# A fused attention, MoE and cosine-MLP kernel: another order for its first cells, other load places, GpSimd work in pieces

## The chip, the cores and the metric

The kernel runs on one core of a Trainium2 chip. The metric is the device time of one execution in microseconds (us). Three runs of the kernel before took 1261.51, 1262.10 and 1262.34 us; the median is 1262.1 us. One further execution was recorded by the hardware profiler.

## The reference

Three layers in a row, all in float32. The first is a linear attention with a decaying state (4 batches, 8 heads, 768 steps, head size 48):

```python
for t in range(S):
    kt, vt, rt = (k[:, :, t], v[:, :, t], r[:, :, t])
    cur = np.einsum('bhd,bhe->bhde', u[None] * kt, vt)
    y[:, :, t] = np.einsum('bhd,bhde->bhe', rt, state + cur)
    state = w[None, :, :, None] * state + np.einsum('bhd,bhe->bhde', kt, vt)
```

Its output, as 3072 tokens of 384 values, goes through a mixture of four experts (`out += p[:, e] * (relu(x @ w1[e]) @ w2[e])`, 1024 wide, p the normalised probabilities) and then through an MLP of width 2048, `(h * cos(h)) @ w_out` with `h = x @ w_in`.

## The kernel before, in words

**Work.** The tokens are cut into six blocks of 512 columns, the hidden layers into units of 8 slices of 128 rows. The program is a list of *items*, numbered n: one weight slice against one token block (256 or 512 columns). An item is an up-projection into a PSUM bank `hp` (two banks, taken in turn, n even and n odd), an evacuation by ScalarE (`gh`, the relu) and VectorE (`gl`, the remainder of the split into two float32r parts), and two items later a down-projection into three banks `a`. Items 0 to 7 use plain float32 with the raw weights (`raw_load(q)` loads those of item q); from item 8 on each product is three float32r matmuls of split operands, so each weight slice is loaded into a staging tile `s` (three of them), then split by ScalarE (high part) and by VectorE or, on odd n, GpSimd (low part). Items 8 to 15 use weight keys 0 to 7; key k is split some items ahead of item 8 + k.

**Attention.** It is cut into 24 *cells* of 128 steps (b, i). The first two are computed ahead of item 0 in a beginning of their own: scores (`b_score`), masks (`b_mask`), products with v (`b_in`), copy to SBUF (`b_y`), transposes to the layout of x (`b_x`). The others are mixed into the items by a table: `ONE_AT[c]` is the item in which cell c's matmuls run (`a_one`), every fourth item up to item 26, every third after it. For each cell p = `ONE_AT[c-1]` sets when the preparing steps are issued: `a_kt` and `a_ru` on GpSimd, `a_r`, `a_rk`, `a_kp` and `a_sum` on VectorE. The matmuls of `a_one` need kp, r, the k table and, since they also write an `hp` bank, the end of the evacuation of the item before. The cell's result goes to DRAM in four stores (`yd`) and comes back as x.

**What sets the order.** Every engine runs its own list in the order in which the program issues it, and a DMA issued by ScalarE stands in ScalarE's list behind the activations before it; the same holds for the loads and stores in SyncE's list. A wait at the head of a list holds everything behind it.

**Names and lines of the steps below.** L728 the dummy matmuls (`warm`), L216 and L225 scores, L239 and L240 mask, L206 `b_ru`, L267 `b_y`, L274 and L275 `b_x` (transposes and the copy to x), L791 and L796 the decay table `table`, `table2`, L589 up-projection of items 0 to 7, L595 to L597 up-projection later, L604 and L608 relu, L609 `gl`, L497 `raw_load`, L493 load of `s`, L504 and L505 weight split, L149 `a_kt`, L153 `a_ru`, L157 `a_rk`, L166 `a_kp`, L161 `a_sum`, L402 the `yd` stores, L693 the GpSimd addition to `acc`.

Of the kernel before, what the change touches and what calls it, by code (L numbers as in the profile page):

```python
# [26 lines left out]
def attention_moe_cos_mlp_kernel(  # L27
# [207 lines left out]
    def b_mask(c):  # L235
        s_ = t_p.tile([128, 2, HP, C], F32, tag="s", name="s")
        by = ld[c]["ps"].rearrange("q c (p a t) -> q a c p t", p=HP, a=2)
        wide = [128, 2, HP, C]
        nc.vector.tensor_tensor(out=s_, in0=by[:, 0], in1=mask.unsqueeze(1).unsqueeze(1).to_broadcast(wide), op=ALU.mult)  # L239
        nc.vector.copy_predicated(  # L240
            out=s_, mask=eye.bitcast(I32).unsqueeze(1).unsqueeze(1).to_broadcast(wide), data=by[:, 1],
        )
        ld[c]["s"] = s_

    def b_in(c, ps):
        d = ld[c]
        tok, s_, so = d["tok"], d["s"], d["so"]
        d["ps_y"] = ps
        for p in range(HP):
            for ch in range(2):  # L250
                for par in range(2):
                    x0, a0 = 64 * (ch ^ par), 64 * ch
                    nc.tensor.matmul(
                        ps[a0:a0 + 64, par, p * D:p * D + D], s_[x0:x0 + 64, ch, p, :], tok[x0:x0 + 64, 4 + ch, p, :],
                        start=p == 0, stop=ch == 0, skip_group_check=True,
                    )
# [239 lines left out]
    def raw_load(q, eng=None):  # L496
        (eng or nc.sync).dma_start(out=raw_w[0, 0, q], in_=moe_wb[q])  # L497

    def w_split(key, eng=None):
        ps, un, q = key  # L500
        t = wp_.tile([128, 2, 2 * DM], F32R, tag="w", name="w")
        if un < NU1:
            src = staged.pop(key)
# [134 lines left out]
    def m_down(n):  # L638
# [10 lines left out]
        def part(t):  # L649
# [128 lines left out]
            double(n)  # L778
            n *= 2

    def tails():
        for a in range(2):
            x = slice(64 * a, 64 * a + 64)
            for ch in range(2):
                last = 2 * C - 1 - C * (ch ^ a)
                nc.scalar.activation(out=tk[x, :, ch], in_=pw[x, :, last:last - C if last >= C else None:-1], func=ACTF.Copy)

    def table():
        pt = ps_d.tile([128, TB], F32, tag="up", name="pt").rearrange("q (p a e) -> q a p e", p=HP, a=2)
# [94 lines left out]
    with tc.manual_schedule():  # L884
# [21 lines left out]
        off = x_bank()
        b_score(0, pair_ps, off[:, 0:HP * C])
        b_off(0)
        tails()
        b_mask(0)  # L910
        b_score(1, dense_ps[0], off[:, HP * C:2 * HP * C])
        b_off(1)
        b_mask(1)
# [2 lines left out]
        b_in(0, dense_ps[1][:, :, 0:HD])
        b_y(0)
        pt = table()
        table2(pt, 0)
        table2(pt, 1)  # L920
        b_in(1, pair_ps[:, :, 0:HD])
        b_y(1)
        b_x(0, dense_ps[0][:, 0])
        b_x(1, dense_ps[0][:, 1])
# [313 lines left out]
```

## Time and profile before

| | |
|---|---|
| median of three runs | 1262.1 us |
| profiled execution, device time | 1262.03 us |
| its span, first to last instruction | 1260.3 us |
| outside the span | 1.73 us |
| granted TensorE clock over the span | 0.999 |

The profile's page gives the busy time of each engine; the view of waits says for which engine's instruction a named engine stood idle; the timeline lists single instructions with start, duration and, in brackets, idle time and its releaser. PE is TensorE, DVE VectorE, ACT ScalarE, POOL GpSimd, SP SyncE; a q behind an engine's name is its queue of DMA issues. Times count from the span's start.

### The profile page before, as it was taken

What the parts mean: (1) busy time and instruction counts of PE and PEld (TensorE: products, weight loads), DVE (VectorE), ACT (ScalarE), POOL (GpSimd) and SP (SyncE); (2) the same over time, 40 slices, a digit from 0 to 9 for tenths busy, and PEclk for the clock granted to TensorE, in tenths of its full rate; (3) what the DMA queues carried; (4) which work ended last, traced back from release to release, by engine and by line L of the source; (5) the groups of instructions that cost most, each with busy time, mean ns of one, the idle gap of its engine ahead of it and who ended that gap; (6) DMA issues with size and microseconds to landing.
All of it is one profiled execution on the core that took longest, in us unless ns stands there. A gap on an engine that the chain in (4) does not pass through costs nothing.

```text
span 1260.3 us, 20498 instructions
## 1 busy us (share of the span) xinstructions
PE 1246.5 (99%) x8453; PEld 1038.8 (82%) x8453; DVE 773.0 (61%) x1259; ACT 492.9 (39%) x879; POOL 193.6 (15%) x190
## 2 busy tenths in 40 slices
PE   9999999999999999999999999999999999999997
PEld 7898888788888888888888888888888888888886
DVE  6897747766264464546645543326776777777665
ACT  4442313223221131112111222216777677767774
POOL 3664323421100000111111111112000100010100
PEclk9999999999999999999999999999999999999999
DMA  8635634444242243223331410123001400160601
GB/s 322 220 117 177 196 125 154 124 137 111 84 139 59 84 134 109 67 76 127 107 92 52 133 43 9 59 78 122 1 1 42 160 26 25 36 203 13 196 11 47
DMA packets 72501, 126.53 MB, mean 100 GB/s; under 512 B 23153, under 2 KB 44754, under 8 KB 72402
## 3 DMA queue, kind: packets, MB, share of 16 engines
q1 hardware_dynamic: 65634, 93.38, 23.6%
q0 software_dynamic: 4608, 25.17, 6.4%
q10 hardware_dynamic: 2160, 6.62, 1.5%
q8 instruction: 67, 1.10, 0.4%
q14 instruction: 32, 0.26, 0.1%
HBM read 101.90 MB, written 23.25 MB: 99 GB/s over the span
## 4 chain that ended last, share of the span: by engine, by line


## 5 line engine op out<-in xcount | busy, mean ns | idle before, releaser
L595 PE MATMUL hp<-xh,w 128*128 128x512 f32 (+1 forms) x888 | 341.3, 384 | 1.6 <-DVE gl L609 1.6
L596 PE MATMUL hp<-xl,w 128*128 128x512 f32 (+1 forms) x888 | 338.1, 381 | 0.5 <-DVE xl L118 0.5
L597 PE MATMUL hp<-xh,w 128*128 128x512 f32 (+1 forms) x888 | 337.9, 380 | 0.2 <-issue 0.2
L670 PE MATMUL a<-gh,w 128*128 128x512 f32 (+1 forms) x880 | 335.0, 381 | 0.0
L671 PE MATMUL a<-gh,w 128*128 128x512 f32 (+1 forms) x880 | 334.8, 380 | 0.0
L672 PE MATMUL a<-gl,w 128*128 128x512 f32 (+1 forms) x880 | 334.7, 380 | 0.0
L608 ACT ACTIVATE gh<-hp 128x512 fp32r<-128x512 f32 (+1 forms) x200 | 114.5, 573 | 539.7 <-PE hp L597 532.6
L609 DVE SCALAR_TENSOR_TENSOR gl<-hp,gh 128x512 fp32r<-128x512 f32 (+1 forms) x200 | 131.1, 657 | 299.5 <-ACT gh L608 298.8
L595 PEld LDWEIGHTS hp<-xh,w 128*128 128x128 f32 x888 | 166.9, 188 | 35.7 <-DVE gl L609 2.9
L597 PEld LDWEIGHTS hp<-xh,w 128*128 128x128 f32 x888 | 166.9, 188 | 32.1
L596 PEld LDWEIGHTS hp<-xl,w 128*128 128x128 f32 x888 | 167.0, 188 | 31.9 <-DVE xl L118 0.7
L670 PEld LDWEIGHTS a<-gh,w 128*128 128x128 f32 x880 | 165.5, 188 | 32.0 <-ACT rr L626 0.4
L672 PEld LDWEIGHTS a<-gl,w 128*128 128x128 f32 x880 | 165.5, 188 | 31.7
L671 PEld LDWEIGHTS a<-gh,w 128*128 128x128 f32 x880 | 165.5, 188 | 31.5
L693 POOL TENSOR_TENSOR acc<-acc,pm 128x512 f32<-128x512 f32 (+1 forms) x57 | 72.5, 1302 | 537.9 <-DVE pm L692 537.9
L628 DVE SCALAR_TENSOR_TENSOR hs<-rr,hs 128x512 f32<-128x512 f32 x96 | 67.4, 702 | 62.8 <-ACT rr L627 62.8
L626 ACT ACTIVATE rr<-rr 128x512 f32<-128x512 f32 x96 | 60.8, 633 | 86.4 <-DVE rr L621 86.4
L620 DVE SCALAR_TENSOR_TENSOR rr<-ni,hs 128x512 f32<-128x512 int32 x96 | 66.3, 691 | 45.6 <-ACT ni L619 45.6
L621 DVE SCALAR_TENSOR_TENSOR rr<-ni,rr 128x512 f32<-128x512 int32 x96 | 66.5, 692 | 3.3
L507 POOL DMA_DIRECT2D w<-dec_all x32 | 17.1, 535 | 333.0 <-PE a L672 332.1
L118 DVE TENSOR_TENSOR gl<-hs,gh 128x512 fp32r<-128x512 f32 x96 | 66.0, 688 | 0.7 <-ACT gh L117 0.7
L618 ACT ACTIVATE hs<-hp 128x512 f32<-128x512 f32 x96 | 57.2, 596 | 17.8 <-PE hp L597 17.6
(151 smaller groups left out, 1066.2 us busy)
## 6 DMA issues: line engine op xcount, KB each, us to landing
w<-dec_all POOLq DMA_DIRECT2D x32, 768.0 KB, 4.6
s<-in_moe_wb_dram SPq DMA_DIRECT2D x53, 384.0 KB, 4.0
draw<-in_moe_wb_dram SPq DMA_DIRECT2D x32, 384.0 KB, 4.3
dec_all<-dout SPq DMA_DIRECT2D x32, 384.0 KB, 3.0
tok<-in_tok_ch_dram SPq DMA_DIRECT2D x19, 576.0 KB, 5.4
rkt<-in_rkt_dram SPq DMA_DIRECT2D x21, 512.0 KB, 3.8
pb<-pn SPq DMA_DIRECT2D x24, 256.0 KB, 5.0
out_dram<-acc SPq DMA_DIRECT2D x17, 256.0 KB, 2.5
```

Source lines behind the costliest of these rows:

```text
L595: nc.tensor.matmul(hp, wh[:, kk, :], x_h[:, kk, :], start=kk == 0, stop=False)
L596: nc.tensor.matmul(hp, wh[:, kk, :], x_l[:, kk, :], start=False, stop=False)
L597: nc.tensor.matmul(hp, wl[:, kk, :], x_h[:, kk, :], start=False, stop=kk == KD - 1)
L608: nc.scalar.activation(out=gh, in_=hp, func=ACTF.Relu)
L609: nc.vector.scalar_tensor_tensor(out=gl, in0=hp, scalar=0.0, in1=gh.bitcast(F32), op0=ALU.max, op1=ALU.subtract)
L620: nc.vector.scalar_tensor_tensor(out=rr, in0=ni, scalar=-PI2_HI, in1=hs, op0=ALU.mult, op1=ALU.add)
L621: nc.vector.scalar_tensor_tensor(out=rr, in0=ni, scalar=-PI2_LO, in1=rr, op0=ALU.mult, op1=ALU.add)
L628: nc.vector.scalar_tensor_tensor(out=hs, in0=rr, scalar=1.0, in1=hs, op0=ALU.subtract, op1=ALU.mult)
L670: nc.tensor.matmul(a, wh[:, ds], gh, start=q == 0, stop=False)
L671: nc.tensor.matmul(a, wl[:, ds], gh, start=False, stop=False)
L672: nc.tensor.matmul(a, wh[:, ds], gl, start=False, stop=q == BLK - 1)
L693: nc.gpsimd.tensor_tensor(out=o, in0=o, in1=m, op=ALU.add)
```

## The change

Five things change.

1. **The beginning.** The two cells' score remainders and the products of the second cell's last two heads get PSUM banks of their own (`off`, `late`); the mask of the second cell and its products are done in two halves; the copies to x are shared between ScalarE and VectorE and stand ahead of `a_r(2)`; the decay table moves into item 1; 13 dummy matmuls instead of 17, and the two dummy matmuls ahead of item 0 become ScalarE copies.
2. **Loads on ScalarE.** None before item 2. The raw weights of item 3 load at item 2 (before: at item 0), those of 4 and 5 at item 3, of 6 at item 4, of 7 at item 5. Cell 3's loads move to item 2. The raw weights of item 2, loaded by SP, go ahead of the probabilities.
3. **Weight splits of keys 0 to 7** come two items later (n - 5 instead of n - 3), their loads with them.
4. **Cell steps.** Cell 2 runs in item 3 (before: 2); `a_rk` runs at p + 1 for cells three items apart, `a_kp` one item later for cells four items apart; the pieces of x of two blocks are spread over other items.
5. **GpSimd in pieces.** `a_kt` two, `a_ru` two, the weight split three, the addition to `acc` one per 256 columns.

```diff
     def a_kt(c, eng=None):
-        t = ld[c]["t"][:, 1]
-        (eng or nc.gpsimd).tensor_tensor(out=t, in0=t, in1=pw[:, :, 127::-1], op=ALU.mult)
+        for h in (slice(0, HP),) if eng else (slice(0, 2), slice(2, HP)):
+            t = ld[c]["t"][:, 1, h]
+            (eng or nc.gpsimd).tensor_tensor(out=t, in0=t, in1=pw[:, h, 127::-1], op=ALU.mult)
...
     ONE_AT = {c: 4 * c - 6 for c in range(N_FIRST, 9)}
+    ONE_AT[N_FIRST] = 3
...
-        yield from ((a_kt, p), (a_r, p + wide), (a_rk, p + 2), (a_kp, p + 2), (a_sum, p + 2 + wide))
+        yield from ((a_kt, p), (a_r, p + wide), (a_rk, p + 1 + wide), (a_kp, p + 2 + wide), (a_sum, p + 2 + wide))
...
-            (eng or nc.vector).tensor_tensor(out=t[:, 1], in0=src, in1=t[:, 0].bitcast(F32), op=ALU.subtract)
+            n = 3 if eng else 1
+            for x in range(n):
+                cols = slice(x * 2 * DM // n, (x + 1) * 2 * DM // n)
+                (eng or nc.vector).tensor_tensor(
+                    out=t[:, 1, cols], in0=src[:, cols], in1=t[:, 0, cols].bitcast(F32), op=ALU.subtract
+                )
...
-            nc.gpsimd.tensor_tensor(out=o, in0=o, in1=m, op=ALU.add)
+            for x in range(0, width(n), 256):
+                nc.gpsimd.tensor_tensor(out=o[:, x:x + 256], in0=o[:, x:x + 256], in1=m[:, x:x + 256], op=ALU.add)
...
-    XT_LAG = 2
+    XT_LAG = 1
-    WARM_FIRST = 17
+    WARM_FIRST = 13
...
         raw_load(1)
+        raw_load(2)
         prob_load()
-        raw_load(2)
...
+        b_mask(0, 0, HP)
+        b_mask(1, 0, 2)
+        b_mask(1, 2, HP)
         a_ru(2)
         a_kt(2)
...
+        late = (x_bank(), ps_d.tile([128, TB], F32, tag="up", name="late"))
+        y0, y1 = dense_ps[1][:, :, 0:HD], pair_ps[:, :, 0:HD]
+        b_in(0, (y0[:, 0], y0[:, 1]), 0, HP)
+        b_y(0, y0, 0, HP)
+        b_in(1, (y1[:, 0], y1[:, 1]), 0, 2)
+        b_y(1, y1, 0, 2)
+        b_in(1, late, 2, HP)
+        b_x(0, dense_ps[1][:, 0], 0, KD)
+        b_x(1, dense_ps[1][:, 1], 0, 1)
+        b_y(1, late, 2, HP)
+        b_x(1, dense_ps[0][:, 0], 1, KD)
+        b_xc(0, dense_ps[1][:, 0], 0, KD, nc.scalar.activation)
+        b_xc(1, dense_ps[1][:, 1], 0, 1, b_copy)
+        b_xc(1, dense_ps[0][:, 0], 1, KD, b_copy)
         a_r(2)
...
-            if n < BLK - 3:
-                raw_load(n + 3, nc.scalar)
-            if 2 <= n < BLK:
-                w_loads(n - 1)
-                w_splits(n - 3, nc.gpsimd if n % 2 else None)
+            for q in {2: (3,), 3: (4, 5), 4: (6,), 5: (7,)}.get(n, ()):
+                raw_load(q, nc.scalar)
+            if 4 <= n < BLK:
+                w_loads(n - 3)
+                w_splits(n - 5, nc.gpsimd if n % 2 else None)
+            if n == 1:
+                pt = table()
+                for a in range(2):
+                    table2(pt, a)
+                for c in range(N_FIRST + 1):
+                    a_kp(c)
...
-                    w_splits(min(BLK * (g + 1) + w_ahead(n, g), n - 3 if n < BLK + 3 else len(w_keys)), nc.gpsimd if n < 28 and n % 2 else None)
+                    w_splits(min(BLK * (g + 1) + w_ahead(n, g), n - 5 if n < BLK + 6 else len(w_keys)), nc.gpsimd if n < 28 and n % 2 else None)
                     w_loads(w_ns[0] + 2)
```

**ScalarE, from the last copy to x to item 2.** Before (`acc_106` is x, `hp_354` and `hp_355` the two up banks, `gh` the relu of an item):

```order
L267 ACTIVATE yo<-pair_ps 128x2x4x48
L275 ACTIVATE acc_106<-ds_ps 128x3x128 x2
L497 DMA raw_xl_101<-in_moe_wb_dram 128x768
L137 DMA tok<-in_tok_ch_dram 128x1152
L128 DMA rkt<-in_rkt_dram 128x1024
L604 ACTIVATE gh<-hp_354 128x256
L497 DMA raw_xh_102<-in_moe_wb_dram 128x768
```

and now (`hp_350`, `hp_351` are the up banks):

```order
L291 ACTIVATE acc_106<-dy_ps 128x3x128
L970 ACTIVATE hp_351<-wu_b 128x256
L627 ACTIVATE gh<-hp_350 128x256
L970 ACTIVATE hp_350<-wu_b 128x256
L820 ACTIVATE wk_ch<-px 64x384 x2
L627 ACTIVATE gh<-hp_351 128x256
L515 DMA raw_xl_101<-in_moe_wb_dram 128x768
L137 DMA tok<-in_tok_ch_dram 128x1152
L128 DMA rkt<-in_rkt_dram 128x1024
L627 ACTIVATE gh<-hp_350 128x256
```

The load of item 3's raw weights (`raw_xl_101`) stood ahead of item 0's relu; it now stands behind item 1's relu, and the loads of cell 3 (`tok`, `rkt`) behind it.

**SyncE, items 6 to 12, up to the second group of `yd` stores (cell 4's, item 10).** Before, the rows with `s` are the loads of weight keys 3 to 7:

```order
L493 DMA s<-in_moe_wb_dram 128x768 x2
L402 DMA yd_605<-yt 48x4x64 x4
L493 DMA s<-in_moe_wb_dram 128x768
L824 DMA pb<-pn 128x4x128 x2
L493 DMA s<-in_moe_wb_dram 128x768
L137 DMA tok<-in_tok_ch_dram 128x1152
L493 DMA s<-in_moe_wb_dram 128x768
L402 DMA yd_605<-yt 48x4x64 x4
L128 DMA rkt<-in_rkt_dram 128x1024
```

and now:

```order
L511 DMA s<-in_moe_wb_dram 128x768
L848 DMA pb<-pn 128x4x128 x2
L511 DMA s<-in_moe_wb_dram 128x768
L137 DMA tok<-in_tok_ch_dram 128x1152
L511 DMA s<-in_moe_wb_dram 128x768
L419 DMA yd_604<-yt 48x4x64 x4
L128 DMA rkt<-in_rkt_dram 128x1024
L511 DMA s<-in_moe_wb_dram 128x768
L432 DMA acc_104<-yd_604 128x3x256
L511 DMA s<-in_moe_wb_dram 128x768
```

Five `s` loads stood ahead of the second group of `yd` stores; now three do, and keys 6 and 7 stand behind those stores.

**VectorE, items 10 to 13, around the relu remainders of items 12 and 13.** Before (`gl<-hp_354` of even, `gl<-hp_355` of odd items; `kp` and `dsum` are of cell 5):

```order
L609 SCALAR_TENSOR_TENSOR gl<-hp_354,gh 128x256
L505 TENSOR_TENSOR w<-s,w 128x768
L145 TENSOR_TENSOR rkt<-rkt,pw 128x512
L609 SCALAR_TENSOR_TENSOR gl<-hp_355,gh 128x256
L157 TENSOR_TENSOR tok<-tok 128x384
L166 TENSOR_TENSOR kp_127<-tok,wk_ch 128x384
L609 SCALAR_TENSOR_TENSOR gl<-hp_354,gh 128x256
L161 TENSOR_REDUCE dsum<-tok 128x8
L609 SCALAR_TENSOR_TENSOR gl<-hp_355,gh 128x256
```

and now (`hp_350` even, `hp_351` odd):

```order
L632 SCALAR_TENSOR_TENSOR gl<-hp_350,gh 128x256
L526 TENSOR_TENSOR w<-s,w 128x768
L145 TENSOR_TENSOR rkt<-rkt,pw 128x512
L632 SCALAR_TENSOR_TENSOR gl<-hp_351,gh 128x256
L159 TENSOR_TENSOR tok<-tok 128x384
L632 SCALAR_TENSOR_TENSOR gl<-hp_350,gh 128x256
L526 TENSOR_TENSOR w<-s,w 128x768
L168 TENSOR_TENSOR kp_127<-tok,wk_ch 128x384
L163 TENSOR_REDUCE dsum<-tok 128x8
L632 SCALAR_TENSOR_TENSOR gl<-hp_351,gh 128x256
```

`kp` stood ahead of item 12's `gl`; it now stands behind it, but with the split of key 6 (the second `w<-s,w`) ahead of `kp` and of item 13's `gl`.

## Rows read from the trace of the kernel before

**Rows 1.** The page: busy time of each engine, share of the span, instructions.

```profile
PE 1246.5 (99%) x8453; PEld 1038.8 (82%) x8453; DVE 773.0 (61%) x1259; ACT 492.9 (39%) x879; POOL 193.6 (15%) x190
```

**Rows 2.** Waits of PE, whole span: who for whom, us in total, times, longest.

```profile
PE hp L595 <- DVE gl L609: 1.6, 3, 1.1
...
PE hp L357 <- DVE gl L609: 1.1, 2, 0.7
PE pair_ps L177 <- DVE kp L166: 0.9, 1, 0.9
PE ds_ps L274 <- ACT acc L275: 0.6, 1, 0.6
PE hp L934 <- ACT acc L275: 0.6, 1, 0.6
PE hp L596 <- DVE xl L118: 0.5, 1, 0.5
```

**Rows 3.** Timeline of PE: start, duration, line, tiles, count.

```profile
1.34 5.80 PE L728 MATMUL hp<-wu_b,wu_a 128*128 128x512 bf16 x17 [1.34 <-DVE wu_b L887]
...
10.98 0.66 PE L791 MATMUL pt<-ident,acc 128*128 128x128 f32 x4
...
12.44 0.28 PE L259 MATMUL pair_ps<-tok,acc 64*64 64x48 f32 x4
...
13.83 0.55 PE L274 MATMUL ds_ps<-ident,yo 128*128 128x128 f32 x3 [0.63 <-ACT acc L275]
14.95 0.38 PE L934 MATMUL hp<-wu_b,wu_a 128*128 128x256 bf16 x2 [0.58 <-ACT acc L275]
15.17 2.75 PE L589 MATMUL hp<-acc,raw_xh 128*128 128x256 f32 x12
...
37.19 0.47 PE L595 MATMUL hp<-xh,w 128*128 128x256 f32 x1
```

**Rows 4.** Timeline of the beginning, ACT.

```profile
6.07 2.45 ACT L206 ACTIVATE acc<-acc,uw 128x128 f32<-128x128 f32 x8 [3.74 <-DVE acc L199]
```

**Rows 5.** Timeline of the beginning, DVE.

```profile
10.45 0.73 DVE L240 COPY_PREDICATED s<-eye,ds_ps 128x512 f32<-128x512 int32 x1
```

**Rows 6.** Raw weights of item 1, one tile's view: the issue, its time to landing.

```profile
L497 SPq DMA_DIRECT2D raw_xh<-in_moe_wb_dram x1: 328/328/328, 7.1 to 7.1; - x1
...
DMA to landing us min/median/max: 8.5/8.5/8.5
```

**Rows 7.** Raw weights of item 3, the same view.

```profile
L497 ACTq DMA_DIRECT2D raw_xl<-in_moe_wb_dram x1: 378/378/378, 14.4 to 14.4; - x1
...
DMA to landing us min/median/max: 3.2/3.2/3.2
```

**Rows 8.** Timeline of ACT at the end of item 0's up-projection.

```profile
16.73 0.38 ACT L604 ACTIVATE gh<-hp 128x256 f32<-128x256 f32 x1 [1.82 <-PE hp L589]
16.75 0.33 ACTq L497 DMA_DIRECT2D raw_xh<-in_moe_wb_dram  x1
```

**Rows 9.** Timeline of DVE around item 14.

```profile
48.30 0.96 DVE L505 TENSOR_TENSOR w<-s,w 128x768 fp32r<-128x768 f32 x1 [0.31 <-ACT w L504]
...
51.56 2.19 DVE L166 TENSOR_TENSOR kp<-tok,wk_ch 128x384 f32<-128x384 f32 x1
53.67 0.41 DVE L609 SCALAR_TENSOR_TENSOR gl<-hp,gh 128x256 fp32r<-128x256 f32 x1
54.01 0.54 DVE L161 TENSOR_REDUCE dsum<-tok 128x8 f32<-128x384 f32 x1
```

**Rows 10.** Timeline of POOL, same stretch.

```profile
51.18 2.16 POOL L505 TENSOR_TENSOR w<-s,w 128x768 fp32r<-128x768 f32 x1
```

**Rows 11.** Timeline of PE, same stretch.

```profile
54.14 0.39 PE L595 MATMUL hp<-xh,w 128*128 128x256 f32 x1 [1.15 <-DVE gl L609]
```

**Rows 12.** Timeline of SP's queue, items 9 to 13.

```profile
41.06 0.38 SPq L493 DMA_DIRECT2D s<-in_moe_wb_dram  x1
47.29 1.78 SPq L402 DMA_DIRECT2D yd<-yt  x4
49.16 1.36 SPq L128 DMA_DIRECT2D rkt<-in_rkt_dram  x1
```

**Rows 13.** All of SP's loads of `s`: time to landing.

```profile
DMA to landing us min/median/max: 2.7/4.0/6.5
```

**Rows 14.** Timeline of ACT, relu of items 12 and 13.

```profile
48.42 0.84 ACT L504 ACTIVATE w<-s 128x768 fp32r<-128x768 f32 x1
49.76 0.39 ACT L608 ACTIVATE gh<-hp 128x256 fp32r<-128x256 f32 x1 [0.49 <-PE hp L597]
51.95 0.39 ACT L608 ACTIVATE gh<-hp 128x256 fp32r<-128x256 f32 x1 [1.81 <-PE hp L597]
```

**Rows 15.** Timeline of DVE ahead of the wait at 236 us.

```profile
233.40 1.64 DVE L157 TENSOR_TENSOR tok<-tok 128x384 f32<-128x384 f32 x1
234.96 1.35 DVE L166 TENSOR_TENSOR kp<-tok,wk_ch 128x384 f32<-128x384 f32 x1
```

**Rows 16.** Timeline of POOL, same stretch.

```profile
230.11 4.51 POOL L693 TENSOR_TENSOR acc<-acc,pm 128x512 f32<-128x512 f32 x3 [3.49 <-DVE pm L692]
```

More of the change, by code (lines that the diff above doesn't have):

```diff
@@ L147, in a_kt @@
     def a_kt(c, eng=None):
-        t = ld[c]["t"][:, 1]
-        (eng or nc.gpsimd).tensor_tensor(out=t, in0=t, in1=pw[:, :, 127::-1], op=ALU.mult)
+        for h in (slice(0, HP),) if eng else (slice(0, 2), slice(2, HP)):
+            t = ld[c]["t"][:, 1, h]
+            (eng or nc.gpsimd).tensor_tensor(out=t, in0=t, in1=pw[:, h, 127::-1], op=ALU.mult)
     def a_ru(c):
-        t = ld[c]["tok"][:, 0:2]
-        nc.gpsimd.tensor_tensor(out=t, in0=t, in1=uu_ch, op=ALU.mult)
+        for ch in range(2):
+            t = ld[c]["tok"][:, ch]
+            nc.gpsimd.tensor_tensor(out=t, in0=t, in1=uu_ch[:, ch], op=ALU.mult)
     def a_rk(c):
@@ L233, in b_off, with b_mask, b_in @@
         ld[c]["so"] = so
-    def b_mask(c):
-        s_ = t_p.tile([128, 2, HP, C], F32, tag="s", name="s")
+    def b_mask(c, p0, p1):
+        if p0 == 0:
+            ld[c]["s"] = t_p.tile([128, HP, 2, C], F32, tag="s", name="s")
+        heads = slice(p0, p1)
+        s_ = ld[c]["s"][:, heads].rearrange("q p c t -> q c p t")
         by = ld[c]["ps"].rearrange("q c (p a t) -> q a c p t", p=HP, a=2)
-        wide = [128, 2, HP, C]
-        nc.vector.tensor_tensor(out=s_, in0=by[:, 0], in1=mask.unsqueeze(1).unsqueeze(1).to_broadcast(wide), op=ALU.mult)
+        wide = [128, 2, p1 - p0, C]
+        nc.vector.tensor_tensor(
+            out=s_, in0=by[:, 0][:, :, heads], in1=mask.unsqueeze(1).unsqueeze(1).to_broadcast(wide), op=ALU.mult
+        )
         nc.vector.copy_predicated(
-            out=s_, mask=eye.bitcast(I32).unsqueeze(1).unsqueeze(1).to_broadcast(wide), data=by[:, 1],
+            out=s_, mask=eye.bitcast(I32).unsqueeze(1).unsqueeze(1).to_broadcast(wide), data=by[:, 1][:, :, heads],
         )
-        ld[c]["s"] = s_
-    def b_in(c, ps):
+    def b_in(c, ps, p0, p1):
         d = ld[c]
         tok, s_, so = d["tok"], d["s"], d["so"]
-        d["ps_y"] = ps
-        for p in range(HP):
+        for p in range(p0, p1):
             for ch in range(2):
@@ L253, in b_in @@
                     nc.tensor.matmul(
[L254 to L255 removed]
+                        ps[par][a0:a0 + 64, p * D:p * D + D], s_[x0:x0 + 64, p, ch, :], tok[x0:x0 + 64, 4 + ch, p, :],
+                        start=p == p0, stop=ch == 0, skip_group_check=True,
                     )
@@ L259, in b_in, with b_y, b_copy, b_x @@
                 nc.tensor.matmul(
-                    ps[64:128, par, p * D:p * D + D], so[x0:x0 + 64, p, :], tok[x0:x0 + 64, 3, p, :],
+                    ps[par][64:128, p * D:p * D + D], so[x0:x0 + 64, p, :], tok[x0:x0 + 64, 3, p, :],
                     start=False, stop=True, skip_group_check=True,
                 )
-    def b_y(c):
-        yo = t_p.tile([128, DM], F32, tag="yo", name="yo", bufs=2)
-        ld[c]["yo"] = yo
+    def b_y(c, ps, p0, p1):
+        if p0 == 0:
+            ld[c]["yo"] = t_p.tile([128, DM], F32, tag="yo", name="yo", bufs=2)
+        yo = ld[c]["yo"][:, p0 * 2 * D:p1 * 2 * D].rearrange("q (p a d) -> q a p d", a=2, d=D)
+        if isinstance(ps, tuple):
+            for a in range(2):
+                (nc.scalar.activation if a == 0 else b_copy)(
+                    out=yo[:, a], in_=ps[a][:, p0 * D:p1 * D].rearrange("q (p d) -> q p d", d=D), func=ACTF.Copy
+                )
+            return
         nc.scalar.activation(
-            out=yo.rearrange("q (p a d) -> q a p d", a=2, d=D),
-            in_=ld[c]["ps_y"].rearrange("q a (p d) -> q a p d", d=D), func=ACTF.Copy,
-        )
-    def b_x(c, px):
-        for kk in range(KD):
+            out=yo, in_=ps[:, :, p0 * D:p1 * D].rearrange("q a (p d) -> q a p d", d=D), func=ACTF.Copy,
+        )
+    def b_copy(out, in_, func):
+        nc.vector.tensor_copy(out=out, in_=in_)
+    def b_x(c, px, k0, k1):
+        for kk in range(k0, k1):
             nc.tensor.transpose(px[:, kk * 128:kk * 128 + 128], ld[c]["yo"][:, kk * 128:kk * 128 + 128], ident)
-        nc.scalar.activation(
-            out=x_raw[:, :, c * 128:c * 128 + 128], in_=px[:, 0:DM].rearrange("q (k t) -> q k t", k=KD), func=ACTF.Copy
+    def b_xc(c, px, k0, k1, copy):
+        copy(
+            out=x_raw[:, k0:k1, c * 128:c * 128 + 128],
+            in_=px[:, k0 * 128:k1 * 128].rearrange("q (k t) -> q k t", t=128), func=ACTF.Copy,
         )
@@ L779, in powers, with tails @@
             n *= 2
-    def tails():
-        for a in range(2):
+    def tails(*halves):
+        for a in halves:
             x = slice(64 * a, 64 * a + 64)
@@ L788, in table @@
     def table():
[L789 removed]
+        pt = x_bank().rearrange("q (p a e) -> q a p e", p=HP, a=2)
         for p in range(HP):
@@ L902, in attention_moe_cos_mlp_kernel @@
             a_kt(c, nc.vector)
-        nc.vector.tensor_tensor(out=w128, in0=pw[:, :, 2 * C:2 * C + 1], in1=pw[:, :, 2 * C:2 * C + 1], op=ALU.mult)
+        tails(0)
         for c in range(N_FIRST):
             b_ru(c)
[L906 to L913, printed above, removed]
+        off = (x_bank(), ps_d.tile([128, TB], F32, tag="up", name="off"))
+        for c in range(N_FIRST):
+            b_score(c, (pair_ps, dense_ps[0])[c], off[c][:, 0:HP * C])
+        for c in range(N_FIRST):
+            b_off(c)
+        tails(1)
+        b_mask(0, 0, HP)
+        b_mask(1, 0, 2)
+        b_mask(1, 2, HP)
         a_ru(2)
         a_kt(2)
[L916 to L924, printed above, removed]
+        late = (x_bank(), ps_d.tile([128, TB], F32, tag="up", name="late"))
[12 more added lines that the diff above has]
+        b_xc(1, dense_ps[0][:, 0], 1, KD, b_copy)
         a_r(2)
+        nc.vector.tensor_tensor(out=w128, in0=pw[:, :, 2 * C:2 * C + 1], in1=pw[:, :, 2 * C:2 * C + 1], op=ALU.mult)
         a_rk(2)
         a_sum(2)
-        for c in range(N_FIRST + 1):
-            a_kp(c)
         ps_d_ctx.close()
@@ L941, in attention_moe_cos_mlp_kernel @@
             moe2 = False
-            if n < BLK - 3:
-                raw_load(n + 3, nc.scalar)
-            if 2 <= n < BLK:
-                w_loads(n - 1)
-                w_splits(n - 3, nc.gpsimd if n % 2 else None)
-            if n == 3:
+            if n < 2:
+                nc.scalar.activation(out=ups2[1 - n][:, 256:512], in_=wu_b[:, 0:256], func=ACTF.Copy)
+            for q in {2: (3,), 3: (4, 5), 4: (6,), 5: (7,)}.get(n, ()):
[5 more added lines that the diff above has]
+                pt = table()
+                for a in range(2):
+                    table2(pt, a)
+                for c in range(N_FIRST + 1):
+                    a_kp(c)
+            if n == 4:
                 prob_norm()
```

9 lines of the change are left out of this document (4 added, 5 removed).

## Prediction

> **What bounds the kernel now.** I read the page's busy shares first: PE works 1246.5 us of a span of 1260.3 us, VectorE 61%, ScalarE 39% [rows 1]. The kernel is bound by TensorE, and the change takes next to nothing out of PE's list that costs time (the dummy matmuls wait for nothing that is computed). So all that it can win is PE's idle time, and all that it can lose is new idle time. The view of waits lists what there is [rows 2]: about 1.2 us for the copies to x ahead of item 0, then 1.6 + 1.1 + 0.9 + 0.5 = 4.1 us for `gl`, `kp` and `xl`. The timeline of PE says where: the beginning up to 15.17, the first matmul of item 0 [rows 3], and 1.15 at 54.14 [rows 11]; the other 2.95 us fall later. Item 8, the first with split weights, starts at 37.19 [rows 3]; what the beginning wins counts only as far as it is still there by then.
>
> **Beginning.** The end of the masks stays: `b_ru` on ScalarE runs 6.07 to 8.52 [rows 4] and still feeds the scores' remainders, and the last mask operation ends at 10.45 + 0.73 = 11.18 [rows 5]; the halves add two operations' overhead, and the scores start a little earlier, so I take 11.1. From there the chain of the second cell is: its last products (about 0.45, as the 0.28 rows around 12.44 stand), copy of y, two transposes (two thirds of 0.55, 0.37), copy to x, item 0. A copy with both handovers is 14.95 - (13.83 + 0.55) = 0.57 [rows 3]. Sum: 11.1 + 0.45 + 0.57 + 0.37 + 0.57 + 0.3 for two engines on one bank and the wait on the slower of two copies = 13.35. That is 15.17 - 13.35 = **-1.8** (bounds -1.2 and -2.2). The table's transposes (0.66), the 0.63 wait for x's copy and the two dummies are what goes. The 13 dummies end about 1.4 us earlier (5.80 / 17 = 0.34 each); a gap of some 0.9 us before the scores is new. [...]
>
> **What loads give back.** Item 0 now starts at 13.35, each item's six matmuls take 1.3 us (a half of 2.75 [rows 3]), and the table (**+0.66**) stands ahead of item 1: wanted at 13.35 + 1.3 + 0.66 = 15.3. But its raw weights land at 7.1 + 8.5 = 15.6 [rows 6], and their issue is not moved: **+0.3** (0 if they land as the next row's do). Then item 1, item 2 and a down-projection, 3 x 1.3: item 3 wants its weights at 19.5. Their load is issued behind item 1's relu, at about 15.6 + 1.3 + 0.25 = 17.15 (an issue goes as soon as the relu ahead begins [rows 8]); with the 3.2 us of the same load before [rows 7] it lands at 20.35: **+0.75**, bounds +0.2 (2.7, the shortest landing of such a load [rows 13]) and +4.1 (6.5). Item 4's load comes one item later with one more in between: **+0.1**. So +1.8 in all, and item 8 starts where it did.
>
> Before, that load was issued at 14.4, ahead of item 0's relu. [...]
>
> **Item 14, the new wait.** Before, PE stood 1.15 us there, since item 13's `gl` (53.67) stood behind a `kp` of 2.19 us [rows 9, 11], which was held by GpSimd's split of 2.16 us [rows 10]. That goes. But the loads of keys 6 and 7, which were issued at about 40 and 41.06, now stand in SP's list behind cell 4's `yd` stores (47.29 + 1.78) and `rkt` (49.16 + 1.36) [rows 12]: issue 49.6 to 50.5. With the median landing of 4.0 [rows 13], key 6 is there at 54.0. ScalarE holds at its split, and with it relu(13), which ran at 51.95 [rows 14]; then ScalarE 0.84 [rows 14], VectorE's split 0.95 and `kp` 0.55 (as the neighbouring row of that width, 0.54) [rows 9]: `kp` is done at 56.35. PE wants it at 53.95 (its wait at 54.14 less 1.15, then about 0.95 of last products and cell work), so it waits 2.4, and up to 0.3 more for `gl(13)`: 2.65 against 1.15, **+1.5**. Bounds: landing 2.7 from 49.6 gives `kp` at 54.65, a wait of 0.7, -0.45; landing 6.5 from 50.5 gives +4.3. Queued behind the wait on ScalarE are relu(13) and key 7's split, on VectorE `kp`, `dsum`, `gl(13)`: all of PE's next item.
>
> **Later waits.** The waits at 62, 87, 108, 236 and 237 us have one pattern: VectorE's two-input operations stretch beside long GpSimd ones (at 233.40, `a_rk` 1.64 and `kp` 1.35 [rows 15] beside three additions of 1.5 each [rows 16]), and `gl` comes late. Pieces of 256 columns or a third of a weight take 0.7 us, so a VectorE operation is held half as long, `a_rk` starts an item earlier and `kp` stands behind `gl`. Of 2.95 us I take **-2.5** (bounds -2.95 and 0, since no row shows two pieces back to back).
>
> The row shows `kp` stretched from 0.55 to 2.19 and ending 0.41 after the GpSimd operation. [...]
>
> Splits of keys 0 to 5 two items later cost nothing: items 8 to 13 come after them by several us, and ScalarE is idle there. The extra GpSimd overhead is covered, POOL being busy 15% [rows 1].
>
> **Sum.** -1.8 + 1.8 + 1.5 - 2.5 = -1.0. The profiled execution took 1262.03 us, 0.07 below the median, so both give **1261.0 us**.
>
> **Rivals.**
> 1. *The loads come in time.* Item 1's and 3's at the short end, key 6's too: -1.8 + 0.66 + 0.2 - 0.45 - 2.5 = -3.9, **1258.1 us**. For it: the shortest landing 2.7, and ScalarE's and SP's lists hold fewer loads side by side then. Against: the median of 4.0, and that `yd` waits for cell 4's result, which nothing makes earlier.
> 2. *Slower: the loads that were moved back land at the long end*, 6.0 us after their issue, as some loads of `s` do (maximum 6.5 [rows 13]), since items 2 to 5 now issue raw weights, cell loads and key loads in a bunch, and items 10 to 12 stores, `rkt` and keys. Item 3 waits until 23.15 (+2.8 more than above), item 14's `kp` comes 2.0 later: -1.0 + 4.8 = +3.8, **1265.8 us**. It decides from about 0.5 us over my landings at both places; below that the sum stays under the time before. Against it: item 3's load is the first of its bunch, so it should land fast.
> [...]
>
> **How the numbers follow.** 0.2% (2.5 us) is about what a measurement can tell from no change: faster is under 1259.6, slower over 1264.6. The forecast has 0.50, with its own range 1259.2 to 1263.0, and 0.10 of that chance under 1259.6; the first rival 0.27, the second 0.11, the third 0.12. Faster 0.27 + 0.10 = 0.37, same 0.40 + 0.12 = 0.52, slower 0.11. The range runs from 1257.4 (the first rival with the beginning at its better bound and `xl` gone, -0.7) to 1263.8 (the third with item 3's load 0.8 later); it leaves out the second rival and a little at the low end.
>
> **What the profile after would show.** Item 0's first matmul at 13.35, within 0.5; PE waiting 0.3 to 1.3 for a DMA of raw weights before items 1 and 3, and item 8 within 0.5 of 37.19. At item 14 PE waits for `kp`, with ScalarE's idle time ahead of key 6's split ended by the DMA of `s`, and relu(13) behind it at about 55. No `kp` over 1.3 us, and the view of waits without lines of 0.5 us or more after 60 us. I am wrong if item 8 starts over 1 us from 37.19, if key 6 lands before 52, or if the granted clock of the first 20 us is below that of before.

## The result and the profile after

The changed kernel takes 1269.35 us (median of six runs, 1268.10 to 1271.35); the kernel before took 1261.96 us in six. The ratio of the two, over all executions, is 1.0053 (95% interval 1.0039 to 1.0066): slower by half a per cent, where 1261.0 us was forecast. The profiled execution has a span of 1266.4 us against 1260.3, so +6.1 us are to be found in it.

The page of the changed kernel: TensorE is as busy as before [rows 1], GpSimd 27 us more in smaller pieces, and queue q8 moved 1.10 MB in 67 packets, 16.4 KB each. I take it for PE's program: 67 packets at 256 instructions (the distance found in run 2) are 17,152, and the page has 16,894 matmuls and weight loads of PE.

```profile
PE 1247.8 (99%) x8447; PEld 1039.0 (82%) x8447; DVE 761.7 (60%) x1264; ACT 492.7 (39%) x881; POOL 220.4 (17%) x301
...
q8 instruction: 67, 1.10, 0.4%
```

The view of waits of PE (who for whom, us in total, times, longest). The `kp` and `hp L357` lines of [rows 2] are gone, the first `gl` line has grown from 1.6 to 1.9 us, four waits for weight splits (`w`) are new, and at the top stands a wait that no engine and no DMA ended:

```profile
PE pair_ps L179 <- issue: 3.9, 1, 3.9
PE hp L618 <- DVE gl L632: 1.9, 3, 1.0
...
PE hp L618 <- ACT w L522: 1.1, 1, 1.1
PE hp L612 <- ACT acc L291: 1.0, 1, 1.0
PE hp L620 <- DVE w L526: 0.9, 2, 0.5
PE hp L620 <- POOL w L526: 0.7, 1, 0.7
...
PE hp L619 <- DVE xl L118: 0.4, 1, 0.4
```

The timeline of PE from item 0 to item 4 (start, duration, line, tiles, count; in brackets idle time and its releaser), against [rows 3]:

```profile
13.99 1.53 PE L612 MATMUL hp<-acc,raw_xh 128*128 128x256 f32 x6 [0.98 <-ACT acc L291]
15.36 0.60 PE L815 MATMUL px<-ident,acc 128*128 128x128 f32 x4
...
20.39 0.67 PE L612 MATMUL hp<-acc,raw_xl 128*128 128x256 f32 x2 [0.54 <-DMA raw_xl<-in_moe_wb_dram]
...
22.22 0.27 PE L179 MATMUL pair_ps<-tok,kp 64*48 64x48 f32 x8
26.41 0.48 PE L179 MATMUL pair_ps<-tok,kp 64*48 64x48 f32 x24 [3.92 <-issue]
...
28.22 2.72 PE L691 MATMUL a<-gh,raw_xh 128*128 128x256 f32 x6
```

Item 0 starts 1.18 us earlier than before, item 3 waits 0.54 us for its weights, and then PE stands 3.92 us in the middle of cell 2's state products: 8 of the 32 are done at 22.5, the other 24, of the same line and the same two tiles, come at 26.41. Before, they ran through:

```profile
19.61 0.55 PE L177 MATMUL pair_ps<-tok,kp 64*48 64x48 f32 x31
```

The six matmuls from 28.22 take 2.72 us where six take 1.46 elsewhere; the granted clock was 0.50 for 3.4 us behind the gap (from 27.35 us). The view of windows in the gap, in the slow stretch and behind it (from and to, length in us, then busy time and count of PE, PEld, DVE, ACT, POOL; granted clock; DMA share; GB/s):

```profile
22.00:26.00 4.00, 0.49 (x36) 0.36 (x28) 1.11 (x2) 0.49 (x1) 0.97 (x2) 1.00 0.69 259
27.50:30.50 3.00, 3.00 (x9) 2.37 (x8) 2.86 (x8) 1.35 (x4) 2.10 (x3) 0.50 0.59 191
31.00:35.00 4.00, 4.00 (x20) 3.54 (x19) 2.48 (x4) 0.88 (x3) 3.50 (x6) 1.00 0.92 320
```

Comparing the starts of equal matmuls in the two traces gives where the time went: -1.2 us at item 0, +5.8 at item 8, +8.3 at item 15, +5.8 at 240 us, +6.6 at the last item.

What ended the gap stands in the DMA queues. Before, the view of DMA queues from 16.5 to 17 us (packets, MB, share) has one piece of PE's program, read from 16.66 to 18.21:

```profile
q10 hardware_dynamic: 69, 0.21, 103.8%
q8 instruction: 1, 0.02, 19.4%
```

In the changed kernel the next piece after 12.2 us is read at 24.14 (same view, 24 to 24.5):

```profile
q10 hardware_dynamic: 65, 0.18, 90.0%
q8 instruction: 1, 0.02, 11.0%
```

and ahead of it ScalarE had issued these in one bunch:

```profile
17.30 0.38 ACTq L515 DMA_DIRECT2D raw_xl<-in_moe_wb_dram  x1
17.72 0.44 ACTq L137 DMA_DIRECT2D tok<-in_tok_ch_dram  x1
18.20 0.44 ACTq L128 DMA_DIRECT2D rkt<-in_rkt_dram  x1
...
18.77 1.14 ACTq L515 DMA_DIRECT2D raw_xh<-in_moe_wb_dram  x2
```

Five loads, 2.3 MB, the last landed at 26.48. PE went on 1.4 us after the piece's read had ended (25.02). Theory F (code): the piece queued behind these loads in the same DMA engines, and PE ran out of program. Rival D (data): the products waited for something that the profile doesn't name. The experiments were made to tell them apart.

### The profile page after: what moved, and what is told of

Same layout as the page of the kernel before. It is cut to its first block, busy times and chain, and to the rows that moved or that the text cites. A ratio compares the mean times of both kernels' runs of the same rounds, so it can differ in the third digit from the quotient of the medians.

```text
span 1266.4 us, 20619 instructions
## 1 busy us (share of the span) xinstructions
PE 1247.8 (99%) x8447; PEld 1039.0 (82%) x8447; DVE 761.7 (60%) x1264; ACT 492.7 (39%) x881; POOL 220.4 (17%) x301
## 4 chain that ended last, share of the span: by engine, by line
## 5 line engine op out<-in xcount | busy, mean ns | idle before, releaser
L717 POOL TENSOR_TENSOR acc<-acc,pm 128x256 f32<-128x256 f32 x108 | 85.9, 831 | 524.8 <-DVE pm L715 524.8
```

The lines of the kernel that those rows point to most:

```text
L717: nc.gpsimd.tensor_tensor(out=o[:, x:x + 256], in0=o[:, x:x + 256], in1=m[:, x:x + 256], op=ALU.add)
```

## Experiments

Each is the kernel named with the edit shown; times are medians.

**1. The bunch spread (e1_spread), changed kernel.**

```diff
-BEGIN = {3: ((a_load_tok, 2), (a_load_t, 2), (a_ru, 3)), ...
+BEGIN = {3: ((a_load_tok, 3), (a_load_t, 3), (a_ru, 4)), ...
-for q in {2: (3,), 3: (4, 5), 4: (6,), 5: (7,)}.get(n, ()):
+for q in {2: (3,), 3: (4,), 4: (5, 6), 5: (7,)}.get(n, ()):
```

> The changed kernel (1269.35 us), but with cell 3's two loads one item later and the raw weights of item 5 at item 4: behind item 1's and item 2's relu ScalarE then issues two loads (raw weights of items 3 and 4) in place of five. Theory F (code): PE's 3.9 us gap at 22.5 to 26.4 is PE out of program; the 16 KB piece read at 24.14, which the kernel before read at 16.66, queued behind those five loads in the same DMA engines. F expects the piece to be read by 22, the gap below 0.7 us, the stretch of lowered clock behind it (about 1.6 us) gone, and 1269.35 - 5.0 = 1264.3 us (1263.3 to 1265.5). Rival D (data): the state products of cell 2 wait for something that a load brings and that the profile does not name. D expects a gap of 3 us or more to stay at that place, since the loads for cell 2 have not moved: 1268 to 1270 us.

Measured 1271.18 us. Timeline of PE:

```profile
24.48 0.48 PE L179 MATMUL pair_ps<-tok,kp 64*48 64x48 f32 x24 [2.00 <-issue]
...
34.72 1.62 PE L612 MATMUL hp<-acc,raw_xh 128*128 128x256 f32 x3 [4.81 <-DMA raw_xh<-in_moe_wb_dram]
```

The piece was read at 22.00, 2.1 us earlier, and the gap fell from 3.92 to 2.00 us, not below 0.7, with two loads still ahead of the read. Under D the gap should have stayed, as nothing of cell 2 moved; it lies between the two forecasts, nearer to F's cause. The time is above the ranges of both: it was lost again at item 5, 4.81 us for raw weights that now stood behind cell loads, with 6.8 us of halved clock from 34.0 us on.

**2. PE's list shifted (e2_narrow), changed kernel, no load moved.**

```diff
+for _ in range(16):
+    nc.tensor.matmul(hp[:, 0:2], wu_a, wu_b[:, 0:2], start=True, stop=True)
-WARM_FIRST = 13
+WARM_FIRST = 10
```

> The changed kernel with its loads untouched, but 16 dummy matmuls of two columns (32 instructions with their weight loads) added to the dummies ahead of the scores and three of the wide dummies taken out: PE's list reaches the same instruction number 26 instructions, about 1.5 us, earlier. F expects PE to ask for the piece before ScalarE's first load of the bunch (17.30), so it is read by about 18, PE has no gap at 22 to 26 and no lowered clock behind it: 1269.35 - 5.5 = 1263.8 us (1262.8 to 1265). D expects no change: 1268.3 to 1270.3 us with the same gap.

Measured 1266.80 us. The gap at the state products is gone, the piece having been read at 17.75. Another gap came one piece earlier, where PE arrived sooner than in the other traces, at 12.1 us, while the piece (11.47 to 12.52) was read hardly earlier than elsewhere:

```profile
13.97 0.38 PE L288 MATMUL dy_ps<-ident,yo 128*128 128x128 f32 x2 [1.88 <-issue]
```

The counts up to the gap (window view, columns as above) in the changed kernel and in this one:

```profile
0.00:24.00 24.00, 19.57 (x345) 13.84 (x345) 14.17 (x36) 10.91 (x28) 4.85 (x16) 1.00 0.76 274
```

```profile
0.00:13.50 13.50, 9.70 (x220) 7.01 (x221) 8.51 (x25) 7.10 (x19) 1.79 (x11) 1.00 0.85 312
```

690 matmuls and weight loads stand ahead of the one gap, 441 ahead of the other. This view leaves out the semaphore instructions in PE's list; with them the traces have 705 and 449, which is 256 apart. In the changed kernel and in runs 1, 3, 4 and 5 PE stopped behind instruction 705 each time. The stop took 1.88 us here and 2.00 to 4.74 us at 705. So PE ran dry at a place in its list, not at an operation, which D cannot say. That the next piece came in time is only in part owed to the 26 instructions: behind the new gap ScalarE's bunch began at 21.77 instead of 17.30. By the medians the gain was 2.6 us rather than 5.5. The profiled execution (1268.86, among the slowest of its ten) gained nothing: it has the new gap, 6.8 us of halved clock behind it and 3.4 us more at 62 us.

**3. The kernel before with 13 dummies (e3_b13).**

```diff
-WARM_FIRST = 17
+WARM_FIRST = 13
```

> The kernel before (1261.96 us) with nothing changed but 13 dummy matmuls instead of 17: 8 instructions fewer, so the piece read at 16.66 is asked for about 1 us later, when ScalarE's loads of 16.75 and 17.97 are under way. F expects it to be read 2 to 5 us later (18.5 to 22), and PE, which needs it after some 700 instructions (at about 18.8 us), to stand 0.5 to 3 us there with issue as the cause: 1262.5 to 1265.5 us. D expects 1261.5 to 1262.5 us and no new gap.

Measured 1266.32 us; the ratio to the kernel before, 1.0014 (0.9997 to 1.0031), does not exclude no change, so the trace has to decide. Of ten executions seven took 1266.0 to 1268.0 us and three 1261.0 to 1262.3. In the profiled one the piece was read at 20.25 instead of 16.66, and PE stood at the same products, again behind instruction 705:

```profile
22.56 0.56 PE L177 MATMUL pair_ps<-tok,kp 64*48 64x48 f32 x12 [3.02 <-issue]
```

```profile
23.00:29.00 6.00, 6.00 (x18) 4.81 (x16) 3.23 (x7) 0.94 (x3) 2.98 (x3) 0.53 0.49 154
```

Four dummy matmuls fewer, and the kernel before has the changed kernel's gap and its halved clock. The median is 0.8 us above the range that F gave; the halved clock, 6.8 us here, was left out of it. That three executions took no longer than before would fit a piece that is sometimes read in time, which is not shown. The kernel before is itself near that edge: PE passed instruction 705 at 19.75, 1.54 us after the read's end, where PE went on 1.4 us after it in the traces with a gap. Of its 26 executions beside this run, six took 1264.2 to 1266.7 us; that the piece came late in them would fit, and is not shown either.

**4. The weight splits alone put back (e4_splits), changed kernel.**

```diff
-if 4 <= n < BLK:
-    w_loads(n - 3)
-    w_splits(n - 5, ...
+if 2 <= n < BLK:
+    w_loads(n - 1)
+    w_splits(n - 3, ...
-... n - 5 if n < BLK + 6 else ...
+... n - 3 if n < BLK + 3 else ...
```

> The changed kernel with the splits of weight keys 0 to 7, and their loads, back two items earlier as in the kernel before. My forecast put +1.5 us on item 14 through the loads of keys 6 and 7 behind the stores; the trace shows +2.4 us over items 9 to 14, four waits of PE for weight splits. If the later splits and loads cause them all, those waits go and the time is 1269.35 - 2.4 = 1267.0 us (1266.3 to 1267.8), with the kp wait of 1.15 us not back because GpSimd works in pieces. If the waits come from the GpSimd pieces of the splits or from the late restart after the gap, they stay: 1268.8 to 1270 us. The gap at 22 us should stay under F and D; one more load now stands in ScalarE's bunch, so under F it may grow by up to 1 us.

Measured 1264.85 us, 4.5 us less by the medians (2.9 between the profiled executions), more than the 2.4 expected. All four waits for splits between 55 and 63 us are gone; between items 8 and 15 the trace gains 3.9 us on the changed kernel's, and it passes item 8 1.5 us later, since one more load in the bunch lengthened the gap as F expected:

```profile
27.31 0.73 PE L179 MATMUL pair_ps<-tok,kp 64*48 64x48 f32 x24 [4.74 <-issue]
```

**5. A shift by 8 instructions (e5_narrow5), changed kernel.**

```diff
+for _ in range(5):
+    nc.tensor.matmul(hp[:, 0:2], wu_a, wu_b[:, 0:2], start=True, stop=True)
-WARM_FIRST = 13
+WARM_FIRST = 12
```

> The changed kernel (1269.35 us) with 5 dummy matmuls of two columns added and one wide one taken out: 8 instructions more ahead of everything, no load moved. In all traces so far PE reads its program in pieces of 16 KB (256 instructions), it passes into the first such piece at instruction 449, and stood dry at 705 (or, with 26 more instructions, at 449); it resumes 1.4 us after a piece's read has ended. Theory F: with 8 more the limit at 449 is passed at about 14.8 instead of 15.6, after its own piece is there (14.7), and the next piece is asked for early enough to be read ahead of ScalarE's bunch, whose first packets go at 18.25. F expects the read before 18.5, no gap at 22.5 and no lowered clock behind it: 1269.35 - 5.5 = 1263.9 us (1263 to 1265). The margin is some tenths of a us; should the read start after 18.3 instead, the gap stays at 2 to 4 us and the time is 1267 to 1269 us. Rival D (an unseen wait for data): 1268.3 to 1270.3 us.

Measured 1268.03 us: the piece was read at 24.12, and the gap stayed at 3.93 us. It moved, though: with 8 instructions more in front, PE stopped four matmuls (with their weight loads, 8 instructions) earlier in the state products, 28 of them left in place of 24:

```profile
26.45 0.56 PE L179 MATMUL pair_ps<-tok,kp 64*48 64x48 f32 x28 [3.93 <-issue]
```

A wait for data would have stayed at its operation. My account of when PE asks for a piece was too exact, as 8 instructions earlier did not bring the read ahead of the bunch. At what instruction it asks stays open; with no load of ScalarE under way, reads came at 17.75 (run 2) and 18.9 to 19.0 (below).

**6. No ScalarE load ahead of the piece (e6_sp3), changed kernel, PE's list untouched.**

```diff
 raw_load(2)
+raw_load(3)
 prob_load()
...
-for q in {2: (3,), 3: (4, 5), 4: (6,), 5: (7,)}.get(n, ()):
+for q in {3: (4, 5), 4: (6,), 5: (7,)}.get(n, ()):
-BEGIN = {3: ((a_load_tok, 2), (a_load_t, 2), (a_ru, 3)), ...
+BEGIN = {3: ((a_load_tok, 3), (a_load_t, 3), (a_ru, 4)), ...
```

> The changed kernel with the raw weights of item 3 on SP behind those of item 2 (issued at about 9.5) and cell 3's two loads behind item 2's relu: ScalarE then issues nothing ahead of about 18.75, no instruction of PE moves. F expects the piece to be read by 18.5, no gap at instruction 705 and no lowered clock, and item 3's wait of 0.54 us gone as well: 1269.35 - 6.0 = 1263.3 us (1262.3 to 1264.5). D expects the gap to stay: 1268 us or more. In items 9 to 14 the four waits for weight splits stay under both.

The gap is gone, with loads moved only; the 32 state products run through, and the piece is read at 19.02, alone in its half microsecond (DMA queues, 19 to 19.5):

```profile
21.73 0.54 PE L179 MATMUL pair_ps<-tok,kp 64*48 64x48 f32 x32
...
32.39 0.92 PE L612 MATMUL hp<-acc,raw_xl 128*128 128x256 f32 x2 [2.58 <-DMA raw_xl<-in_moe_wb_dram]
```

```profile
q8 instruction: 1, 0.02, 13.2%
```

That settles F for the gap, as far as ScalarE's loads delay the read; that the two share DMA engines is not shown. By its time alone the run would have passed for D's: 1268.16 us is 3.7 above F's range. It hardly fell, as cell loads now stood ahead of item 6's raw weights, 2.58 us, and the clock fell again behind that wait (the 32 matmuls of L193 took 1.14 us at 33.24 against 0.66 at 21.25); most executions were slower than the profiled one (1266.09).

**7. The same with the splits put back (e7_sp3_splits)** (edits of 6 and 4, the loads from item 3 on).

> The kernel of the run before it, and in addition the splits of weight keys 0 to 7 and their loads two items earlier (first loads at item 3). Taking the splits back alone was worth 1269.35 - 1264.85 = 4.5 us, of which its trace shows 2.4 at items 9 to 14. If the two are independent, 1263.3 - 2.4 = 1260.9 us (1260 to 1262), below the kernel before (1262.0). If the two key loads more in ScalarE's list behind item 2's relu delay item 5's weights or cell 3, 0.5 to 2 us are given back: up to 1263 us.

Measured 1267.32 us; the read at 18.93, no gap, no wait for splits, but the waits for the loads pushed back are larger (waits of PE):

```profile
PE pair_ps L179 <- DVE kp L168: 3.4, 1, 3.4
PE hp L612 <- DMA raw_xl<-in_moe_wb_dram: 3.2, 1, 3.2
```

**8. The same with whole GpSimd operations (e8_sp3_splits_nopiece).**

```diff
-n = 3 if eng else 1
+n = 1
-for x in range(0, width(n), 256):
-    nc.gpsimd.tensor_tensor(out=o[:, x:x + 256], in0=o[:, x:x + 256], in1=m[:, x:x + 256], op=ALU.add)
+nc.gpsimd.tensor_tensor(out=o, in0=o, in1=m, op=ALU.add)
...
```

> The kernel of the run before it, with GpSimd's operations whole again. My forecast gave the pieces, with kp behind gl and rk an item earlier, 2.5 us in the waits of 60 to 240 us, and the trace shows 2.5. If the pieces bring most of it: slower by 1.5 to 2.5 us than the run before it, with waits for gl and kp back near 60 to 110 and at 236 us. If the reordering of kp and rk brings it: within 0.5 us of the run before it. If the pieces cost (POOL's busy time rose by 27 us, and PE waits 0.4 to 0.5 for gl at 360 and 618 us are longer than before): faster by 0.3 to 1 us.

Measured 1269.84 us, 2.5 us more. From 68 to 240 us its trace falls back by 4.3 us against run 7's (a `kp` wait of 1.48 us at 97.3 and 3.4 us of halved clock behind it, `gl`, `xl`), and from there to the end it wins 0.7 back, as the waits for `gl` near 358 and 616 us are shorter without pieces.

**9. Loads where there is room (e9_early), changed kernel.** The edits of 7, and cell 3's loads at item 0, cell 4's one item later.

```diff
+BEGIN = {3: ((a_load_tok, 0), (a_load_t, 0), (a_ru, 3)), 4: ((a_load_tok, 4), (a_load_t, 5), (a_ru, 6)), ...
```

> The changed kernel with: splits and loads of keys 0 to 7 two items earlier (first loads at item 3); the raw weights of item 3 on SP; cell 3's two loads at item 0 as in the kernel before (issued at about 14.4, read by about 18.4), cell 4's one item later. With splits back alone the trace still showed 4.74 us of PE without program, 3.4 us through the lowered clock behind it and 0.77 us of waits for raw weights (1264.85 us). F expects the piece read at 18.5 to 19.5, just in time for instruction 705 (reached at about 21.8, so a read up to 19.4 costs nothing, later ones as much as they are later), and with ScalarE's list shorter the weights of items 5 and 6 and kp of cell 3 in time: 1264.85 - 8.9 + 0.5 = 1256.5 us (1255.5 to 1258.5). If the two cell loads ahead of the piece push it to 20.5, 1 us of gap and up to 1.7 us of lowered clock come back: 1259 us.

Measured 1258.59 us, ratio to the kernel before 0.9961 (0.9945 to 0.9976). The piece was read at 18.96, there is no gap at 22 us and no halved clock ahead of the last 5 us, and item 8 starts at 37.29, 0.1 us from [rows 3]. The time is 0.1 us beyond my range: PE still waits for x's copies and for `gl`, and a stop of 0.39 us at 49.97, behind instruction 1473 (449 and four times 256), is a later piece:

```profile
PE hp L618 <- DVE gl L632: 1.0, 3, 0.5
PE hp L612 <- ACT acc L291: 1.0, 1, 1.0
...
PE hp L619 <- issue: 0.4, 1, 0.4
```

**10. One part alone: the kernel before with GpSimd in pieces, and `rk` and `kp` at the new items (e10_bpieces).**

```diff
-(a_rk, p + 2), (a_kp, p + 2),
+(a_rk, p + 1 + wide), (a_kp, p + 2 + wide),
```

and the four pieces of the change's diff.

> The kernel before (1262.0 us) with only GpSimd's operations in pieces and rk and kp at the new items; PE's instructions and all loads stay, so the piece at 16.66 is read as before. My forecast gave this part 2.5 us, and the changed kernel's trace as well as the run with whole operations (+2.5 us) agree: 1262.0 - 1.0 (kp's wait at item 14, most of 1.15) - 2.0 = 1259.0 to 1260.0 us. If the part needs the later splits or the spread x copies to bring it, less than 1 us: 1261.2 to 1262.2.

Measured 1257.28 us, ratio 0.9947 (0.9926 to 0.9967), the best of all and 1.7 us below the expected range. `gl` waits fall from 2.7 us in [rows 2] to 1.0, `kp` and `xl` waits are gone:

```profile
PE hp L179 <- ACT gh L611: 1.1, 1, 1.1
...
PE hp L602 <- DVE gl L616: 0.5, 2, 0.4
PE hp L359 <- DVE gl L616: 0.5, 1, 0.5
```

The profiled execution was the slowest of its six (1258.84) and carries a wait of 1.1 us at 19.5 that none of the other traces has: one DMA issue on ScalarE took 2.46 us there. At the last item its trace is 3.3 us ahead of the trace before, with 1.3 us lost between items 2 and 3 around that wait.

## Why the prediction was wrong

**What bounds the kernel.** Right: what was lost is idle time of PE (3.9 us at the state products), and a lowered clock behind it (0.50 for 3.4 us).

**Beginning.** Sized too high: -1.2 instead of -1.8. The step "two engines on one bank", whose 0.3 was an estimate with no row behind it, failed: the copies did not run side by side. The timeline of DVE shows its first copy held 0.82 us until ScalarE's from the same tile (`dy_ps`) is done, and PE waits 0.98 us; and the last mask operation ended at 11.30, not 11.1:

```profile
13.27 0.29 DVE L284 COPY acc<-dy_ps 128x128 f32<-128x128 f32 x1 [0.82 <-ACT acc L291]
13.47 0.41 DVE L284 COPY acc<-ds_ps 128x256 f32<-128x256 f32 x1
```

**What loads give back.** The steps named were near: table 0.60, item 1 no wait (0.3 expected), item 3 0.54 (0.75 expected), its load issued at 17.30 and landed 2.95 us later. The step that failed is its conclusion, "item 8 starts where it did". I followed every data transfer past the moved issues and not the one that no line of the kernel issues, PE's own program. It came 7.5 us later, and cost a gap of 3.9 us and 1.7 us of halved clock: 5.6 us, where the span grew by 6.1 and the other terms nearly cancel. The loads account for some 5.1 of the 7.5 us, as run 6, with none ahead, reads at 19.02; why not at 16.66 even there stays open. No rival had it; the slower rival had late loads as its mechanism, but at item 3, where little happened, and at key 6. Its sign was visible: q8 has a line of its own on the page, and the loads that the change gathers behind the relus of items 1 and 2 are five.

**Item 14.** The mechanism was right up to the split, and wrong in what PE waits for. Key 6's load stood behind the `yd` stores (timeline of SP) and landed 5.1 us after its issue (4.0 in the sum), ScalarE's split waited for it 4.0 us, relu(13) stood behind it, then VectorE's split and `kp`:

```profile
53.12 1.78 SPq L419 DMA_DIRECT2D yd<-yt  x4
...
55.51 1.48 SPq L511 DMA_DIRECT2D s<-in_moe_wb_dram  x1
```

```profile
60.66 0.84 ACT L522 ACTIVATE w<-s 128x768 fp32r<-128x768 f32 x1 [4.00 <-DMA s<-in_moe_wb_dram]
61.41 0.37 ACT L631 ACTIVATE gh<-hp 128x256 fp32r<-128x256 f32 x1
```

```profile
61.53 0.96 DVE L526 TENSOR_TENSOR w<-s,w 128x768 fp32r<-128x768 f32 x1 [4.18 <-ACT w L522]
62.41 0.55 DVE L168 TENSOR_TENSOR kp<-tok,wk_ch 128x384 f32<-128x384 f32 x1
```

`kp` took 0.55 us as estimated; the long one of [rows 9] is gone. But PE never waited for it: item 14's up-projection, which comes first, needs key 6 itself, and PE waited for its high part and then its low part (the last two rows below). And "splits of keys 0 to 5 two items later cost nothing" failed: the first two rows are waits for keys 4 and 5 at items 12 and 13.

```profile
55.14 0.38 PE L620 MATMUL hp<-xh,w 128*128 128x256 f32 x1 [0.43 <-DVE w L526]
...
58.26 0.39 PE L620 MATMUL hp<-xh,w 128*128 128x256 f32 x1 [0.71 <-POOL w L526]
...
61.55 0.39 PE L618 MATMUL hp<-xh,w 128*128 128x256 f32 x1 [1.12 <-ACT w L522]
...
62.55 0.38 PE L620 MATMUL hp<-xh,w 128*128 128x256 f32 x1 [0.49 <-DVE w L526]
```

Items 8 to 15 lost 2.4 us net, where 1.5 were forecast. With the splits and loads put back (run 4) the same items win 1.4 us on the kernel before: the later splits and loads cost 3.9 us, and the rest of the change won 1.4.

**Later waits.** Right in sum: -2.4 us between item 15 and 240 us, -2.5 forecast, though a `gl` wait of 1.04 us stands at 113.92; run 8 shows that whole operations bring such waits back. That VectorE gets in between two pieces, and the 0.12 for the case that it does not, were my estimates; in the trace the longest `kp` is 1.10 us, at 240.65 beside six pieces of 5.33 us together, against 2.19 before [rows 9] and a median of 0.55. Not forecast were 0.8 us of `gl` waits from 350 us on, where run 8 loses less: additions in pieces also had a price here.

**The clock.** The gap ahead of the scores did not come: the 13 dummies took 5.68 us, where 17 took 5.80 [rows 3], the scores start at 6.95, and the granted clock is 1.00 from 7 to 20 us. It fell to 0.50 behind the gap at item 3 instead.

## What to carry to other kernels

When a change gathers loads or moves them, look also for the reads of the program in that stretch: here the piece was read at 16.66 us in the kernel before and at 24.14 behind five loads, and PE stood 3.92 us in a run of 32 short matmuls. A gap in the middle of a run of equal instructions with "issue" as its cause, and a `q8 instruction` packet that ended 1.4 us ahead of its end, was its mark in six traces; such gaps lay 256 instructions, or a multiple, apart in PE's list. And test the parts of a change apart: here the GpSimd pieces with `rk` and `kp` were worth -5.2 us by the medians (1257.28 against 1262.46), while the later loads and splits cost 10.8 us (1269.35 against run 9's 1258.59).

## What the runs showed of the hardware

- PE went on 1.4 us after the read of a missing piece ended, in all six traces with such a gap (1.38 to 1.45 us), and 1.28 to 1.45 us after it at three shorter stops (0.38 to 0.58 us, runs 5, 9 and 10). All nine stand behind instruction 449 of PE's list or a multiple of 256 further on.
- The second piece was read at 17.75 to 19.0 us where no load of ScalarE was under way (runs 2, 6 and 7), at 22.0 behind two loads (run 1), at 24.1 behind five (the changed kernel) and at 25.0 behind six (run 4). In the kernel before it was read at 16.66 with three of ScalarE's loads issued at 14.4 to 15.3; the read took 1.55 us, and 3.3 us in run 10, against 0.9 to 1.2 us for the same piece in the other traces.
- With gaps of PE of 2.6 to 4.8 us the granted clock fell to 0.5, within the gap or up to 1.9 us behind its end, and stayed there for 3.4 to 6.8 us. The gap of 2.00 us in run 1 had none of this, while in run 2 gaps of 1.88 and 1.06 us close together had, and in run 8 one of 1.48 us.
- Four dummy matmuls fewer cost the kernel before 4.0 us by the medians and 5.5 us at the last item of the two traces (run 3); the trace shows the gap at the piece and the halved clock.
